# Six zero products in the opening of a fused attention and maxout kernel

## The chip, the cores and the metric

The kernel runs on one core of a Trainium2 chip. The metric is the device time of one execution in microseconds, the median of several runs. A core has five engines with a list of instructions each: TensorE (PE: matrix products into PSUM, with a weight load, PEld, ahead of each), VectorE (DVE), ScalarE (ACT), GpSimd (POOL) and SyncE (SP, which here issues the transfers). An engine works through its list in order and waits on semaphores for the others.

## The reference

Gated linear attention with a state of 48 x 48 for each head, and behind it a maxout layer; B, H, S, D = 4, 8, 768, 48:

```python
f = 1.0 / (1.0 + np.exp(-f_logit))
for t in range(S):
    state = f[:, :, t, :, None] * state + np.einsum('bhd,bhe->bhde', k[:, :, t], v[:, :, t])
    y[:, :, t] = np.einsum('bhd,bhde->bhe', q[:, :, t], state)
# x: y as 3072 tokens x 384
h1 = x @ w1            # 384 x 1024
h2 = x @ w2            # 384 x 1024
out = np.maximum(h1, h2) @ w_out   # 1024 x 384
```

## The kernel before

The 768 steps are cut into 3 windows of 256, and a piece is one window of one batch entry: 12 pieces, numbered 0 to 11. The steps inside a piece are turned into matrix products over chunks of 64. The maxout is computed as h2 + relu(h1 - h2), so the weights become wd = w1 - w2, and m2 = w2 @ w_out, worked out in the kernel itself, takes the place of h2 followed by w_out.

What runs when is written out by hand in the string ORDER. Each word is a step: letters for the kind, then the piece (and a part of it), then a letter for the engine (a ScalarE, v VectorE, p GpSimd, s SyncE), and after @ a PSUM bank or a slot of SBUF. The words are executed in order, and each engine's list holds its steps in that order. The waits are put in from what reads and writes the same bank or tile, so a product that rewrites a bank waits until the last reader of that bank is done.

The kinds that matter for the opening, with the line by which the profile names them:

- Lf, Lk, Lq, Lv: loads of f_logit, k, q, v of a piece (L124); Wa, Wb, Wo: loads of w1, w2, w_out (L137, L140, L144). All are issued by SP in ORDER's sequence.
- E, F, G: ScalarE's exp, ln, exp of the gate (L215 gate, L219 ell, L223 one); e: the sum of log gates in bf16 (L226).
- C: TensorE's running sum of e, one product of 384 columns (L230) and four of 2 columns (L233); X, Z: exp of it (L240, L245).
- i, j, K, Q, V: scaled k, q and the bf16 v (L249, L253, L260, L263; V, as all copies, is L113).
- t, u: TensorE's transposes of k and q (L278), U their copies out of PSUM (L113).
- A: scores of a piece, half at a time, 16 products (L315); m: VectorE's mask on them (L321).
- D: the state's addition, 32 products (L379); n, N: the state's update (L396, L398, L401).
- S, y: the two parts of the piece's output, from the state and from the masked scores (L336). Between them stands z (look, L113): a copy of one column of the banks that S wrote and that y adds into.
- Y: the output's copy xT (L113); wc, wt, wx: cast, transpose (L463) and copy of w2; wo: cast of w_out; wm: m2's 24 products (L478); wn its copies; ws: wd (L488).
- d: x times wd (L418), r: relu (L427), o: the last products (L440).

A kind h exists too, and ORDER does not use it. The tile zeros, a slot of SBUF that nothing else writes, is set to 0 at the start (L149):

```python
    zeros = slots[:, ZEROS, 0:256].bitcast(BF16)
    nc.vector.memset(slots[:, ZEROS, 0:256], 0.0)
...
    def step_h(n, b):
        for _ in range(n):
            nc.tensor.matmul(out=banks[:, b, :], lhsT=zeros[:, 0:C], rhs=zeros, start=True, stop=True)
```

The steps are then called by the words:

```python
    for word in ORDER.split():
        key, of, e, b = re.fullmatch(r"([A-Za-z]+)([0-9.]+)([avps]?)@?([0-9]*)", word).groups()
        steps[key](*map(int, of.split(".")), e, int(b or 0))
```

Of the kernel before, what the change touches and what calls it, by code (L numbers as in the profile page):

```python
# [17 lines left out]


ORDER = """  # L20
Lf1s@22 E1 F1 e1p Lf0s@14 E0 F0 Lk1s@10 C1@3 G1 e0v i1v Lq1s@3 C0@0 X1 Lq0s@23 Lv1s@17 V1p Z1 Z0 j1v Q1v
Lk0s@0 u1@2 Wb0s K1v Wb2s Wb1s t1@7 X0 G0 j0v i0p Lv0s@3 Q0v g2v U1.0a@7 D1@3 U1.1a@2 wc0a wc2p u0@7 Wo1s
n1.0@2 K0v U0.1v@7 Wo2s A1.0@1 m1.0@1 n1.1@2 wt0@3 t0@0 A1.1@1 wc1p wx0v@3 S1.0@6 Wo3s Wo0s wt2@4 Lf3s@16
m1.1@1 U0.0a@0 wt1@3 z1v@6 g0v wo1p V0a wo3p wx2a@4 A0.0@0 y1 m0.0@0 wx1a@3 wo2a S1.1@6 D0@0 n0.0@0 E3
A0.1@3 Wa1s n0.1@1 F3 Y1.0v@6 S0.0@4 Lf2s@11 Wa0s N1.1p wo0p m0.1@3 z0a@4 Lq2s@26 Lk3s@10 wm1@0 Y1.1a@7 e3v
wm3@0 wm2@0 wm0@0 y0 S0.1@4 Lq3s@22 Lk2s@19 wn2a@2 C3@2 ws2v g4p wn0a@0 Y0.1v@5 Y0.0a@4 ws3v E2 wn1v@1
Lf4s@3 Lv3s@24 Lf5s@15 d1.2@6 F2 e2v ws1v N0.1v ws0v Lv2s@0 d0.2@3 d0.3@4 d1.3@7 Z3 G3 r0.1a@3 j2v C2@5
d0.1@1 r1.1a@6 d1.1@4 Z2 X3 Q2v d1.0@3 V3p d0.0@0 r1.0a@3 i3v X2 K3v r0.0a@0 g6v G2 o1.0@6 Lq4s@4 j3v o0.0@4
Q3v u3@2 t3@2 i2v b1.0.0a@6 K2v u2@6 U3.2v@2 Lf6s@14 t2@6 b0.0.0v@4 o0.1@0 U2.0v@6 U2.1a@7 E4 D3@1 b0.1.0a@0
Lk5s@5 F4 n3.0@0 e4p A3.0@3 A3.1@6 o1.1@5 m3.0@3 E5 A2.1@0 S3.0@2 z3a@2 b1.1.0a@5 V2p m3.1@6 n3.1@0 A2.0@6  # L30
m2.0@6 y3 S3.1@2 D2@4 F5 Lk4s@15 n2.0@1 e5p C4@7 j4v Y3.2a@2 S2.0@5 Lq6s@8 g3v n2.1@2 Z4 Lv4s@9 Lq5s@2
m2.1@0 d3.1@2 G5 X4 Lf7s@23 z2a@5 Lk6s@0 G4 d3.2@3 g5p d3.3@4 y2 Q4p S2.1@5 C5@0 Lv5s@20 i4p d3.0@1 E6 F6
g1p Y2.2a@5 i5v Lf8s@26 r3.1v@3 Lq7s@27 e6v K4v Lk7s@7 d2.3@6 r3.0a@1 Lv6s@11 d2.2@5 X5 d2.0@2 j6v C6@1
d2.1@3 r2.1a@5 X6 V4a Lf9s@25 G6 u4@6 Z6 N3.1v t4@6 o3.1@4 U4.2v@6 D4@5 N2.1v r2.0a@2 Lv9s@15 A4.0@2 Z5
Lv7s@22 K5p j5v A4.1@0 o2.1@7 m4.0@2 Q5p b3.1.0a@4 E7 m4.1@0 F7 Lq8s@3 n4.0@1 i6p N4.0v V5a K6p b2.1.0a@7
n4.1@2 u5@2 t5@2 o2.0@4 G7 E8 U5.2v@2 F8 o3.0@5 S4.0@6 b3.0.0a@5 A5.0@2 z4v@6 Q6p m5.0@2 D5@0 S4.1@6
b2.0.0a@4 N4.1p y4 Lk9s@0 Y4.2a@6 Lk8s@20 A5.1@4 n5.0@2 e8p Lf10s@17 t6@2 u6@2 C8@0 m5.1@4 d4.1@7 N5.0p e7p
Lq10s@26 n5.1@0 d4.0@6 i7p X8 d4.3@1 Z8 r4.0a@6 U6.2v@2 j7v C7@3 Z7 V6p X7 Lv8s@6 d4.2@0 Lq9s@2 r4.1a@0
S5.0@6 E9 Lk11s@23 z5v@6 A6.0@4 D6@2 m6.0@4 F9 y5 n6.0@2 V7a K7p G9 N6.0v N5.1p S5.1@6 Lk10s@1 e9p A6.1@0 G8
o4.1@4 Y5.2v@6 d5.1@2 C9@7 b4.1.0a@4 m6.1@0 j8v d5.2@5 Q7p d5.3@6 d5.0@1 r5.0a@1 i8p E10 o4.0@0 n6.1@1  # L40
Lf11s@10 Lv10s@25 F10 r5.1v@5 G10 S6.0@1 K8p D7@4 z6v@1 n7.0@0 S6.1@1 g7p y6 u7@3 N7.0p Lq11s@17 t7@3 Q8v X9
Y6.2a@1 N6.1p Z9 b4.0.0a@0 Tk8s o5.0@6 n7.1@2 Tq8s e10v C10@5 V8v j9v d6.2@0 j10v U7.2a@3 Z10 d6.0@2
b5.0.0a@6 X10 d6.1@3 i9p r6.0a@2 d6.3@1 r6.1a@0 Q9v i10p Tq9s Q10v o5.1@4 K9v b5.1.0a@4 E11 A7.0@6 A7.1@0
D8@2 V9p S7.0@4 F11 m7.0@6 n8.0@0 o6.1@3 m7.1@0 V10p b6.1.0a@3 z7a@4 o6.0@2 b6.0.0a@2 D9@7 K10v Tk9s S7.1@4
y7 n9.0@1 D10@3 e11v A8.0@6 N9.0p Y7.2a@4 m8.0@6 A8.1@0 C11@2 d7.0@4 N7.1p d7.1@5 m8.1@0 X11 j11v d7.2@6 Z11
# [511 lines left out]
```

## Time and profile before

| what | before |
| --- | --- |
| median of 3 runs | 137.16 us |
| lowest and highest run | 136.89, 137.48 us |
| the profiled execution, its own time | 137.17 us |
| its span, first to last instruction | 135.4 us |
| busy in the span: PE / DVE / ACT / POOL | 120.2 / 95.6 / 83.8 / 53.5 us |
| weight loads (PEld), beside PE | 89.7 us |
| PE busy from 7 to 16 us, from 16 to 20, from 20 to 24 | 5.29 of 9, 4.00 of 4, 3.01 of 4 us |

Times in the profile count from the start of the span. PE's busy time merges overlapping products: a product's row runs from its start until its result is there, and the next one may start before. How fast a sequence of products goes is therefore read from one start to the next. A row of the timeline merges neighbours of a kind: the start, the time until the last one ends, the engine, the line, the output and inputs, the shape, how many, and in brackets the idle time before it with what ended that. The chain of waits follows the execution back from its last instruction, at each step to what released it.

### The profile page before, as it was taken

The page shows a single profiled execution, that of the slowest core. Times are in us where ns is not written, and L with a number is a line of the kernel's source. Part 1 is how long each engine was busy: PE and PEld are TensorE (multiplying, and loading weights), DVE is VectorE, ACT ScalarE, POOL GpSimd, SP SyncE. Part 2 cuts the span into 40 slices and gives each one's busy share as a digit, 9 for nine tenths or more (in the row PEclk, how much of TensorE's full clock was granted, in tenths as well). Part 3 has the DMA queues.
Part 4 walks back from the last instruction along what each step waited for, and adds up shares of the span by engine and source line. Part 5 has one row for each costly group of instructions (what it writes and reads, how often), then busy time and mean ns, then how long its engine had stood idle before and what let it go on. Part 6 is the DMA issues. An engine that isn't in the chain of part 4 may idle for free.

```text
span 135.4 us, 5468 instructions
## 1 busy us (share of the span) xinstructions
PE 120.2 (89%) x2415; PEld 89.7 (66%) x2415; DVE 95.6 (71%) x149; ACT 83.8 (62%) x132; POOL 53.5 (40%) x60
## 2 busy tenths in 40 slices
PE   0037797999999999999999999999999999999991
PEld 0016685667666788665977877667878677885570
DVE  6469885579998999988989949995894691030320
ACT  3693676399829699995689299863846012641421
POOL 5112552600012595399779976924291100000000
PEclk9999999999999999999999999999999999999999
DMA  3999999999999999999998999999929993020062
GB/s 96 273 261 294 392 356 337 320 345 241 251 262 268 263 259 250 266 261 248 250 238 207 278 262 236 249 160 204 110 82 228 389 351 134 0 116 0 18 242 94
DMA packets 62216, 30.77 MB, mean 227 GB/s; under 512 B 58736, under 2 KB 59120, under 8 KB 62192
## 3 DMA queue, kind: packets, MB, share of 16 engines
q1 hardware_dynamic: 62192, 30.41, 89.9%
q8 instruction: 19, 0.31, 1.0%
q14 instruction: 5, 0.04, 0.1%
HBM read 23.59 MB, written 4.72 MB: 209 GB/s over the span
## 4 chain that ended last, share of the span: by engine, by line
PE 79%; SPq 6%; DVE 6%; DMA 4%; ACT 2%; issue 1%; DVEq 0%
PE banks L440 33%; PE banks L418 22%; PE banks L336 9%; SPq L124 6%; DMA slots<-in_moe_w_dram 4%; PE banks L315 4%; PE banks L478 3%; DVE at_m L321 3%; PE banks L285 3%; PE banks L379 2%; ACT slots L113 2%; PE banks L230 2%; PE banks L463 1%; DVE wd L488 1%; PE banks L278 1%
## 5 line engine op out<-in xcount | busy, mean ns | idle before, releaser
L440 PE MATMUL banks<-wo,gT 128*128 128x384 bf16 (+1 forms) x200 | 35.2, 320 | 0.0
L418 PE MATMUL banks<-xT,wd 128*128 128x256 bf16 x288 | 34.1, 273 | 0.1
L321 DVE TENSOR_TENSOR at_m<-banks,mask 128x1024 bf16<-128x1024 f32 x24 | 28.9, 1218 | 3.1 <-PE banks L315 2.1
L418 PEld LDWEIGHTS <-wd 128*128 128x128 bf16 x288 | 27.1, 98 | 4.3 <-DVE wd L488 0.5
L440 PEld LDWEIGHTS <-gT 128*128 128x128 bf16 x200 | 19.1, 98 | 12.1 <-ACT gT L427 0.6
L427 ACT ACTIVATE gT<-banks 128x1024 bf16<-128x1024 f32 (+1 forms) x21 | 20.4, 985 | 9.1 <-PE banks L418 8.3
L113 ACT COPY slots<-banks 128x384 f32<-128x384 f32 (+2 forms) x22 | 11.2, 524 | 15.5 <-PE banks L440 15.4
L440 PE MATMUL banks<-m,xT 128*128 128x384 bf16 (+1 forms) x75 | 15.9, 321 | 0.1
L113 POOL CAST vb<-slots 128x768 bf16<-128x768 f32 x7 | 8.0, 1150 | 19.1 <-DMA slots<-in_v_dram 19.1
L429 DVE TENSOR_SCALAR gT<-banks 128x1024 bf16<-128x1024 f32 (+1 forms) x5 | 4.9, 1006 | 13.4 <-ACT slots L113 7.2
L215 ACT ACTIVATE gate<-slots 128x768 f32<-128x768 f32 x12 | 10.2, 846 | 5.1 <-DMA slots<-in_f_logit_dram 5.1
L249 POOL TENSOR_TENSOR slots<-slots,one 128x384 f32<-128x384 f32 x8 | 9.7, 1211 | 4.7 <-ACT one L223 2.6
L230 PE MATMUL banks<-e,u_inc 128*128 128x384 bf16 x12 | 4.3, 356 | 8.0 <-POOL e L226 7.4
L336 PE MATMUL banks<-at_m,vb 64*64 64x128 bf16 x576 | 10.7, 217 | 0.0
L219 ACT ACTIVATE ell<-gate 128x768 f32<-128x768 f32 x12 | 10.1, 846 | 0.5
L401 POOL TENSOR_TENSOR state<-tmp_s,dec 128x192 bf16<-128x192 f32 x10 | 5.9, 606 | 10.8 <-DVE tmp_s L396 10.8
L260 POOL TENSOR_TENSOR kp<-slots,inv 128x768 bf16<-128x768 f32 x5 | 9.1, 1815 | 2.6 <-ACT inv L240 1.5
L113 ACT COPY trs<-banks 128x1024 bf16<-128x1024 bf16 (+1 forms) x5 | 5.8, 1191 | 6.8 <-PE banks L278 4.3
L336 PEld LDWEIGHTS <-vb 64*64 64x64 bf16 x576 | 9.3, 106 | 0.5 <-issue 0.5
L336 PE MATMUL banks<-trs,state 48*64 48x128 bf16 x240 | 9.0, 222 | 0.3 <-DVE state L398 0.2
L315 PE MATMUL banks<-trs 48*64 48x128 bf16 x384 | 9.3, 225 | 0.0
L263 DVE TENSOR_TENSOR qp<-slots,dec 128x768 bf16<-128x768 f32 x8 | 9.0, 1136 | 0.3
(68 smaller groups left out, 178.2 us busy)
## 6 DMA issues: line engine op xcount, KB each, us to landing
slots<-in_f_logit_dram SPq DMA_DIRECT2D x12, 384.0 KB, 6.0
slots<-in_k_dram SPq DMA_DIRECT2D x12, 384.0 KB, 6.4
slots<-in_q_dram SPq DMA_DIRECT2D x12, 384.0 KB, 6.3
slots<-in_v_dram SPq DMA_DIRECT2D x12, 384.0 KB, 6.2
out_dram<-slots SPq DMA_DIRECT2D x11, 384.0 KB, 3.7
slots<-in_moe_w_dram SPq DMA_DIRECT2D x3, 512.0 KB, 6.0
slots<-in_moe_w_out_dram SPq DMA_DIRECT2D x4, 384.0 KB, 8.6
slots<-in_moe_w_dram SPq DMA_DIRECT2D x2, 768.0 KB, 7.4
```

The lines of the kernel that those rows point to most:

```text
L113: (nc.scalar.copy if e == "a" else engines[e].tensor_copy)(out, in_)
L215: nc.scalar.activation(flat(gate[s]), flat(loaded[s]["f"]), AF.Exp, bias=0.0, scale=-1.0)
L219: nc.scalar.activation(flat(ell[s]), flat(gate[s]), AF.Ln, bias=1.0, scale=1.0)
L249: engines[e].tensor_mul(even, even, one[s])
L260: engines[e].tensor_mul(pad("kp", s)[:, :, :, 0:D], by_parity(loaded[s]["k"]), both(inv[s]))
L263: engines[e].tensor_mul(pad("qp", s)[:, :, :, 0:D], by_parity(loaded[s]["q"]), both(dec[s][:, 0:HD].rearrange("p (h d) -> p h d", h=H)))
L315: nc.tensor.matmul(out=ps[h * HC:(h + 1) * HC, j % 2, par, :], lhsT=chunk(s, 0, rows, j, h)[:, par, :], rhs=chunk(s, 1, rows, j, h), start ...
L321: nc.vector.tensor_mul(at[s][:, jj].rearrange("p r j a t -> p (r j) (a t)"), banks[:, b:b + 2, :].rearrange("p r (j x) -> p (r j) x", j=2) ...
L336: nc.tensor.matmul(out=ys[s][h][c * DP:(c + 1) * DP, blk // 2, :], lhsT=lhs[:, at_col + off:at_col + off + DP], rhs=rhs, start=(s, h, c) n ...
L418: nc.tensor.matmul(out=ps[:, f, :], lhsT=wd[:, fp, kt, f * C:(f + 1) * C], rhs=xT[g][:, kt, :], start=(kt == 0), stop=(kt == KT - 1))
L427: nc.scalar.activation(dst, src, AF.Relu)
L440: nc.tensor.matmul(out=ps, lhsT=lhs, rhs=rhs[:, out_cols], start=(i == 0), stop=(i == len(terms) - 1))
```

## The change

ORDER gets three words more: h3@5 behind C0 (the first pieces' running sum), h1@5 behind t1 (the transposes of piece 1's k), and h2@5 behind A1.0 (the first half of piece 1's scores). Each is so many products of the zero tile with itself, 128 rows by 512 columns, into PSUM bank 5. No step reads what they write; bank 5 is written by S0.0 afterwards. The other words are the same in the same order, only broken into lines in another way:

```diff
-Lf1s@22 E1 F1 e1p Lf0s@14 E0 F0 Lk1s@10 C1@3 G1 e0v i1v Lq1s@3 C0@0 X1 Lq0s@23 Lv1s@17 V1p Z1 Z0 j1v Q1v
-Lk0s@0 u1@2 Wb0s K1v Wb2s Wb1s t1@7 X0 G0 j0v i0p Lv0s@3 Q0v g2v U1.0a@7 D1@3 U1.1a@2 wc0a wc2p u0@7 Wo1s
-n1.0@2 K0v U0.1v@7 Wo2s A1.0@1 m1.0@1 n1.1@2 wt0@3 t0@0 A1.1@1 wc1p wx0v@3 S1.0@6 Wo3s Wo0s wt2@4 Lf3s@16
...
+Lf1s@22 E1 F1 e1p Lf0s@14 E0 F0 Lk1s@10 C1@3 G1 e0v i1v Lq1s@3 C0@0 h3@5 X1 Lq0s@23 Lv1s@17 V1p Z1 Z0 j1v
+Q1v Lk0s@0 u1@2 Wb0s K1v Wb2s Wb1s t1@7 h1@5 X0 G0 j0v i0p Lv0s@3 Q0v g2v U1.0a@7 D1@3 U1.1a@2 wc0a wc2p
+u0@7 Wo1s n1.0@2 K0v U0.1v@7 Wo2s A1.0@1 h2@5 m1.0@1 n1.1@2 wt0@3 t0@0 A1.1@1 wc1p wx0v@3 S1.0@6 Wo3s Wo0s
...
```

Two of the three places, in TensorE's list. Behind t1, the transposes of kp (piece 1's k), D1 followed directly before, with a wait of its weight load for ScalarE and of its product for GpSimd's cast of v:

```order
L278 LDWEIGHTS kp_101
L278 MATMUL banks<-ident,kp_101 128x128
L379 LDWEIGHTS kp_101 [waits Activation_49]
L379 MATMUL banks<-vb_113,kp_101 64x48 [waits Pool_49]
L379 LDWEIGHTS kp_101
```

and now one zero product stands between them, with no wait of its own:

```order
L278 LDWEIGHTS kp_101
L278 MATMUL banks<-ident,kp_101 128x128
L492 LDWEIGHTS slots
L492 MATMUL banks<-slots 128x512
L379 LDWEIGHTS kp_101 [waits Activation_49]
L379 MATMUL banks<-vb_113,kp_101 64x48 [waits Pool_49]
```

Behind A1.0 (trs: the transposed k and q) the first transposes of w2 followed before, which wait for ScalarE's cast of w2 (slots) and for VectorE:

```order
L315 LDWEIGHTS trs_208
L315 MATMUL banks<-trs_208 64x128
L463 LDWEIGHTS slots [waits Activation_49]
L463 MATMUL banks<-ident,slots 128x128 [waits DVE_49]
L463 LDWEIGHTS slots
```

and now two zero products come first (the numbers behind the names of tiles are counted anew):

```order
L315 LDWEIGHTS trs_212
L315 MATMUL banks<-trs_212 64x128
L492 LDWEIGHTS slots
L492 MATMUL banks<-slots 128x512
L492 LDWEIGHTS slots
L492 MATMUL banks<-slots 128x512
L463 LDWEIGHTS slots [waits Activation_49]
L463 MATMUL banks<-ident,slots 128x128 [waits DVE_49]
```

The three behind C0 stand in the same way ahead of the first transposes of qp, which wait for VectorE. The lists of VectorE, ScalarE, GpSimd and SP hold the same steps in the same order as before.

More of the change, by code (lines that the diff above doesn't have):

```diff
@@ L20 @@
 ORDER = """
-Lf1s@22 E1 F1 e1p Lf0s@14 E0 F0 Lk1s@10 C1@3 G1 e0v i1v Lq1s@3 C0@0 X1 Lq0s@23 Lv1s@17 V1p Z1 Z0 j1v Q1v
-Lk0s@0 u1@2 Wb0s K1v Wb2s Wb1s t1@7 X0 G0 j0v i0p Lv0s@3 Q0v g2v U1.0a@7 D1@3 U1.1a@2 wc0a wc2p u0@7 Wo1s
-n1.0@2 K0v U0.1v@7 Wo2s A1.0@1 m1.0@1 n1.1@2 wt0@3 t0@0 A1.1@1 wc1p wx0v@3 S1.0@6 Wo3s Wo0s wt2@4 Lf3s@16
-m1.1@1 U0.0a@0 wt1@3 z1v@6 g0v wo1p V0a wo3p wx2a@4 A0.0@0 y1 m0.0@0 wx1a@3 wo2a S1.1@6 D0@0 n0.0@0 E3
-A0.1@3 Wa1s n0.1@1 F3 Y1.0v@6 S0.0@4 Lf2s@11 Wa0s N1.1p wo0p m0.1@3 z0a@4 Lq2s@26 Lk3s@10 wm1@0 Y1.1a@7 e3v
@@ L26 @@
[L26 to L40, printed above, removed]
@@ L41 @@
-Lf11s@10 Lv10s@25 F10 r5.1v@5 G10 S6.0@1 K8p D7@4 z6v@1 n7.0@0 S6.1@1 g7p y6 u7@3 N7.0p Lq11s@17 t7@3 Q8v X9
-Y6.2a@1 N6.1p Z9 b4.0.0a@0 Tk8s o5.0@6 n7.1@2 Tq8s e10v C10@5 V8v j9v d6.2@0 j10v U7.2a@3 Z10 d6.0@2
+Lf1s@22 E1 F1 e1p Lf0s@14 E0 F0 Lk1s@10 C1@3 G1 e0v i1v Lq1s@3 C0@0 h3@5 X1 Lq0s@23 Lv1s@17 V1p Z1 Z0 j1v
+Q1v Lk0s@0 u1@2 Wb0s K1v Wb2s Wb1s t1@7 h1@5 X0 G0 j0v i0p Lv0s@3 Q0v g2v U1.0a@7 D1@3 U1.1a@2 wc0a wc2p
+u0@7 Wo1s n1.0@2 K0v U0.1v@7 Wo2s A1.0@1 h2@5 m1.0@1 n1.1@2 wt0@3 t0@0 A1.1@1 wc1p wx0v@3 S1.0@6 Wo3s Wo0s
@@ new lines @@
+wt2@4 Lf3s@16 m1.1@1 U0.0a@0 wt1@3 z1v@6 g0v wo1p V0a wo3p wx2a@4 A0.0@0 y1 m0.0@0 wx1a@3 wo2a S1.1@6 D0@0
+n0.0@0 E3 A0.1@3 Wa1s n0.1@1 F3 Y1.0v@6 S0.0@4 Lf2s@11 Wa0s N1.1p wo0p m0.1@3 z0a@4 Lq2s@26 Lk3s@10 wm1@0
+Y1.1a@7 e3v wm3@0 wm2@0 wm0@0 y0 S0.1@4 Lq3s@22 Lk2s@19 wn2a@2 C3@2 ws2v g4p wn0a@0 Y0.1v@5 Y0.0a@4 ws3v E2
+wn1v@1 Lf4s@3 Lv3s@24 Lf5s@15 d1.2@6 F2 e2v ws1v N0.1v ws0v Lv2s@0 d0.2@3 d0.3@4 d1.3@7 Z3 G3 r0.1a@3 j2v
+C2@5 d0.1@1 r1.1a@6 d1.1@4 Z2 X3 Q2v d1.0@3 V3p d0.0@0 r1.0a@3 i3v X2 K3v r0.0a@0 g6v G2 o1.0@6 Lq4s@4 j3v
@@ new lines @@
+o0.0@4 Q3v u3@2 t3@2 i2v b1.0.0a@6 K2v u2@6 U3.2v@2 Lf6s@14 t2@6 b0.0.0v@4 o0.1@0 U2.0v@6 U2.1a@7 E4 D3@1
+b0.1.0a@0 Lk5s@5 F4 n3.0@0 e4p A3.0@3 A3.1@6 o1.1@5 m3.0@3 E5 A2.1@0 S3.0@2 z3a@2 b1.1.0a@5 V2p m3.1@6
+n3.1@0 A2.0@6 m2.0@6 y3 S3.1@2 D2@4 F5 Lk4s@15 n2.0@1 e5p C4@7 j4v Y3.2a@2 S2.0@5 Lq6s@8 g3v n2.1@2 Z4
+Lv4s@9 Lq5s@2 m2.1@0 d3.1@2 G5 X4 Lf7s@23 z2a@5 Lk6s@0 G4 d3.2@3 g5p d3.3@4 y2 Q4p S2.1@5 C5@0 Lv5s@20 i4p
+d3.0@1 E6 F6 g1p Y2.2a@5 i5v Lf8s@26 r3.1v@3 Lq7s@27 e6v K4v Lk7s@7 d2.3@6 r3.0a@1 Lv6s@11 d2.2@5 X5 d2.0@2
@@ new lines @@
+j6v C6@1 d2.1@3 r2.1a@5 X6 V4a Lf9s@25 G6 u4@6 Z6 N3.1v t4@6 o3.1@4 U4.2v@6 D4@5 N2.1v r2.0a@2 Lv9s@15
+A4.0@2 Z5 Lv7s@22 K5p j5v A4.1@0 o2.1@7 m4.0@2 Q5p b3.1.0a@4 E7 m4.1@0 F7 Lq8s@3 n4.0@1 i6p N4.0v V5a K6p
+b2.1.0a@7 n4.1@2 u5@2 t5@2 o2.0@4 G7 E8 U5.2v@2 F8 o3.0@5 S4.0@6 b3.0.0a@5 A5.0@2 z4v@6 Q6p m5.0@2 D5@0
+S4.1@6 b2.0.0a@4 N4.1p y4 Lk9s@0 Y4.2a@6 Lk8s@20 A5.1@4 n5.0@2 e8p Lf10s@17 t6@2 u6@2 C8@0 m5.1@4 d4.1@7
+N5.0p e7p Lq10s@26 n5.1@0 d4.0@6 i7p X8 d4.3@1 Z8 r4.0a@6 U6.2v@2 j7v C7@3 Z7 V6p X7 Lv8s@6 d4.2@0 Lq9s@2
@@ L43 @@
+r4.1a@0 S5.0@6 E9 Lk11s@23 z5v@6 A6.0@4 D6@2 m6.0@4 F9 y5 n6.0@2 V7a K7p G9 N6.0v N5.1p S5.1@6 Lk10s@1 e9p
+A6.1@0 G8 o4.1@4 Y5.2v@6 d5.1@2 C9@7 b4.1.0a@4 m6.1@0 j8v d5.2@5 Q7p d5.3@6 d5.0@1 r5.0a@1 i8p E10 o4.0@0
+n6.1@1 Lf11s@10 Lv10s@25 F10 r5.1v@5 G10 S6.0@1 K8p D7@4 z6v@1 n7.0@0 S6.1@1 g7p y6 u7@3 N7.0p Lq11s@17 t7@3
+Q8v X9 Y6.2a@1 N6.1p Z9 b4.0.0a@0 Tk8s o5.0@6 n7.1@2 Tq8s e10v C10@5 V8v j9v d6.2@0 j10v U7.2a@3 Z10 d6.0@2
 b5.0.0a@6 X10 d6.1@3 i9p r6.0a@2 d6.3@1 r6.1a@0 Q9v i10p Tq9s Q10v o5.1@4 K9v b5.1.0a@4 E11 A7.0@6 A7.1@0
```

## The prediction

> **What bounds the kernel now.** I read the page first, then the chain of waits, then the opening instruction by instruction, because the change touches nothing later.
>
> ```profile
> span 135.4 us, 5468 instructions
> ...
> PEclk9999999999999999999999999999999999999999
> ```
>
> The profiled execution took 137.17 us, 1.77 more than its span, and the runs' median is 137.16; a sum made on this span needs no correction. The clock row says full speed everywhere. Below, the durations contradict it for the opening.
>
> The chain of waits, from 14 to 33 us (start, length, what):
>
> ```profile
> 8.81 5.97 DMA slots<-in_moe_w_dram
> ...
> 15.97 1.03 PE banks L463 x8
> ...
> 20.79 1.24 DVE at_m L321
> 22.02 0.04 issue
> 22.07 0.33 PE banks L379 x17
> ...
> 23.76 4.01 PE banks L478 x24
> ...
> 29.26 0.56 DVE xT L113
> ...
> 31.62 0.88 DVE wd L488
> ```
>
> Until 15.97 a load of weights and its cast set the time, then TensorE (the transposes), then exchanges of VectorE and TensorE, then 24 products (L478), then VectorE up to 32.5. What follows is TensorE's. Busy time by stretch (stretch, its length, PE busy, the other engines, clock, DMA):
>
> ```profile
> 33.00:46.00 13.00, 13.00 (x258) 8.78 (x259) 11.89 (x18) 8.70 (x16) 2.61 (x3) 1.00 1.15 255
> 48.00:79.00 31.00, 30.72 (x684) 22.95 (x686) 27.75 (x35) 24.82 (x42) 25.17 (x22) 1.00 1.05 251
> 80.00:97.00 17.00, 17.00 (x357) 12.80 (x348) 14.98 (x19) 12.82 (x22) 9.24 (x9) 1.00 1.13 194
> 100.00:132.00 32.00, 32.00 (x490) 23.95 (x488) 12.60 (x19) 10.10 (x16) 2.54 (x3) 1.00 0.45 156
> ```
>
> PE idles 0.28 us in these 93. So the end moves by what the opening moves the products at 32.55, and by nothing else.
>
> Now TensorE in the opening (timeline: start, length, line, shapes, count, idle before):
>
> ```profile
> 8.49 0.48 PE L230 MATMUL banks<-e,u_inc 128*128 128x384 bf16 x1 [0.56 <-DVE e L226]
> ...
> 10.72 1.03 PE L278 MATMUL banks<-ident,qp 128*128 128x128 bf16 x8 [1.67 <-DVE qp L263]
> 11.60 1.04 PE L278 MATMUL banks<-ident,kp 128*128 128x128 bf16 x8
> 12.97 0.63 PE L379 MATMUL banks<-vb,kp 64*64 64x48 bf16 x32 [0.34 <-POOL vb L113]
> 13.79 1.03 PE L278 MATMUL banks<-ident,qp 128*128 128x128 bf16 x8 [0.19 <-DVE qp L263]
> 14.76 0.64 PE L315 MATMUL banks<-trs 48*64 48x128 bf16 x16
> 15.97 1.03 PE L463 MATMUL banks<-ident,slots 128*128 128x128 bf16 x8 [0.58 <-ACT slots L113]
> 16.80 1.06 PE L278 MATMUL banks<-ident,kp 128*128 128x128 bf16 x8
> 17.79 0.64 PE L315 MATMUL banks<-trs 48*64 48x128 bf16 x16
> ...
> 20.25 0.42 PE L315 MATMUL banks<-trs 48*64 48x128 bf16 x16
> ```
>
> The same 16 products of L315 take 0.64 us at 14.76 and 17.79, and 0.42 at 20.25. Eight transposes take 0.83 (15.97 to 16.80), or 0.104 each. TensorE runs slowly first. The rise lies late in the second group of L463: these stretches (that line alone) meet as many transposes in half the time.
>
> ```profile
> 19.50:19.90 0.40, 0.40 (x7) 0.40 (x5) 1.00 0.99 384
> 19.92:20.12 0.20, 0.20 (x7) 0.20 (x4) 1.00 1.52 543
> ```
>
> And PE alone, over two neighbouring stretches up to the rise:
>
> ```profile
> 13.09:16.50 3.41, 2.65 (x62) 1.00 1.01 402
> 16.50:19.92 3.42, 3.42 (x47) 1.00 1.12 343
> ```
>
> With holes (2.65 of 3.41) the clock did not rise; after an unbroken run, from 15.97, it did. That is the bound the traces give: an unbroken run of more than 1.9 us (10.72 to 12.64 was not enough) and at most 3.9.
>
> **The change, part by part.** Nothing is removed, no wait is added, no other engine's or queue's list changes. Added are six products of 512 columns, each with a weight load. No row has 512 columns; from the transposes, 128 columns slow are 0.104, so one costs 4 x 0.104 = 0.42 slow; from 24 products of 384 columns in 4.01 (0.167 each) one costs 0.22 fast.
>
> The three behind C0 start about 9.0 and end by 10.3, before the transposes at 10.72 that wait for VectorE: nothing. The one behind t1 runs from about 12.5 to 12.95; D1 behind it waits for GpSimd until 12.97: 0 to 0.2 late, and D1 would still end ahead of 13.79, where the next transposes wait for qp: nothing. The two behind A1.0 start at about 15.35 (its last products begin before 15.1 and end at 15.40). Slow they last until 16.2, so L463 starts 0.2 late; fast they end at 15.8, in the hole of 0.58. If the products leave the clock as it is, the sum is therefore +0.2.
>
> If they count as work, TensorE is busy from 10.72 on save the 0.19 before 13.79. An unbroken 3.9 us ends at 14.6 if that hole doesn't matter, at 17.7 if it starts the count anew. I follow the gain from there to 32.55, with these rows (all engines):
>
> ```profile
> 16.14 1.22 DVE L321 TENSOR_TENSOR at_m<-banks,mask 128x1024 bf16<-128x1024 f32 x1
> 17.54 0.68 DVE L113 COPY slots<-banks 128x1024 bf16<-128x1024 bf16 x1
> 18.48 1.23 DVE L321 TENSOR_TENSOR at_m<-banks,mask 128x1024 bf16<-128x1024 f32 x1 [0.27 <-PE banks L315]
> ...
> 23.26 0.83 POOL L113 CAST wo<-slots 128x768 bf16<-128x768 f32 x1 [2.56 <-DMA slots<-in_moe_w_out_dram]
> ...
> 25.72 0.84 ACT L215 ACTIVATE gate<-slots 128x768 f32<-128x768 f32 x1 [2.62 <-DMA slots<-in_f_logit_dram]
> 26.65 0.84 ACT L219 ACTIVATE ell<-gate 128x768 f32<-128x768 f32 x1
> 27.40 0.14 ACT L113 COPY look<-banks 128x1 f32<-128x1 f32 x1
> 27.53 0.56 DVE L226 TENSOR_TENSOR e<-ell 128x384 bf16<-128x384 f32 x1 [2.12 <-ACT look L113]
> 27.69 0.89 PE L336 MATMUL banks<-at_m,vb 64*64 64x128 bf16 x48
> 28.00 0.95 DVE L488 TENSOR_TENSOR wd<-slots 128x768 bf16<-128x768 f32 x1
> 28.69 0.34 PE L230 MATMUL banks<-e,u_inc 128*128 128x384 bf16 x1
> 29.26 0.56 DVE L113 CAST xT<-banks 128x384 bf16<-128x384 f32 x1 [0.30 <-PE banks L233]
> ```
>
> (1) The 16 transposes from 15.97 would save up to half of 1.7 us. But A1.1 (17.79) rewrites banks that m1.0 on VectorE reads until 17.36: it starts at 17.4, 0.4 earlier. (2) m1.1 (18.48) then follows the copy that ends at 18.22: 0.26 earlier, ending at 19.45. (3) A0.0 (20.25) writes a bank that m1.1 reads, so it starts at 19.5, 0.77 earlier; the transposes of wt2 and wt1, fast, are done by then. m0.0 (20.79), D0 (22.07) and the 24 products keep these 0.77: 22.9 instead of 23.69. (4) The second six need a cast that GpSimd begins when its load lands, 23.26 + 0.83 = 24.09. Unhindered they would start at 23.9; they start at 24.13. Gain left: 0.55; the products end at 27.2. (5) y0 (27.69) adds into the banks that look (ACT, 27.40) has to read first. Look stands in ScalarE's list behind gate and ell, which start when a load of f_logit lands at 25.7, issued at 15.3 and not moved by the change. So y0 goes on at 27.58: gain left 0.11. (6) Past it, VectorE's e waits for the same ell (27.49), and wd (28.00) stands behind e; wd ends at 28.95 as before. xT (29.26) is put down to the end of C3, whose products follow y0; with 0.11 off these, xT starts at 29.15. From there VectorE's list up to 31.62 + 0.88 has no idle place, and the products at 32.55 follow it: 0.11 earlier. If the 0.30 before xT has another cause, it is 0. I take 0.1, as the row names PE: 137.17 - 0.1 = 137.05, rounded. Of the 0.77 of step (3) a seventh is left, because one load decides at 25.7.
>
> The Trainium skill, in "TensorE: Matmul & The Clock Gate", Part 4, speaks against the change: a transpose does not count as work for the clock in the way that a product does. By it the zero products, with little but transposes between them, would raise nothing, which is the first rival. The rows bear it out poorly: the run in which the clock rose, 15.97 to 19.9, consists mostly of transposes. The same page, Part 1, says that the clock rises after one busy window of about 3.4 us, and that the windows run on freely; the two stretches above agree with it. By that rule the rise could come at a different moment in each execution, and the sum stays the same for all moments up to 17.7.
>
> **The rivals.** *No earlier rise.* The products do not count, or the holes still break the run. Then L463 starts 0.2 late and the chain passes it on through 20.79, 23.76 and 29.26: 137.17 + 0.2 = 137.4. For it: 2.65 of 3.41 busy was not enough, and the hole at 13.6 stays. Against: six products fill 1.3 us of holes, and the largest, 0.58, lies just ahead of the unbroken run, which then would start at 13.79.
>
> *The load is not the bound in other executions.* y0 waits for look by only 0.15 (27.54 to 27.69). Should f_logit land 0.5 us earlier in an execution that isn't profiled, steps (5) and (6) give way and the 0.55 of step (4) comes through: 137.17 - 0.55 = 136.6. The runs' spread, 136.89 to 137.48, is of such a size; against it, the profiled execution lies on the median.
>
> *Slower: the clock falls back.* Faster products leave more idle time between 16 and 23, since VectorE's times stay. From the point where some 3.4 us hold too little work, the clock drops again, and the 24 products meet it: half speed over 3.4 us loses 1.7 of work. Less the 0.55 gained, y0 starts 1.15 later: 138.3. Against it, the holes of 0.5, 0.24 and 0.2 us between 21.5 and 23.4 do not slow the products behind them now.
>
> **How the numbers follow.** The forecast, 137.05, has 0.62; no earlier rise 0.17; the load not binding 0.14; the fall 0.05; 0.02 is left for what I do not see. A measurement of this kernel tells a difference from none at about 0.5%, 0.69 us. The forecast and the first rival lie inside; of the second some lies beyond, where all 0.77 of step (3) survive. That makes 0.86 for no difference, 0.07 faster, 0.07 slower. The range is the first rival's 137.4 and the second's 136.6, each with about 0.1 for the spread of a median: 136.5 to 137.5. The forecast's own range, 0 to 0.11 gained and the same spread, is 136.95 to 137.3.
>
> **What would show it.** Right: L315 at 14.76 or at 17.4 takes about 0.42, the 24 products of L478 begin near 22.9 and pause near 24, gate still begins at 25.7 behind its load, and wd at 28.0 and L418 at 32.5 stand where they stood. Step (1) is wrong if L315 still takes 0.64 at its second place; step (5) if y0 begins before look has ended or gate begins earlier; step (6) if xT keeps its 0.30. The forecast falls if the L418 products at 32.55 move by more than 0.4 either way, or if PE idles after 33.

## The result, and the profile after

The change made the kernel slower: 138.03 us (137.69 to 138.35) against 137.09 (136.84 to 137.48) in runs on the same chip, a ratio of 1.007 with a 95% interval of 1.0054 to 1.0087. The profiled execution took 137.69 us, 0.52 more than that of before. Of two kernels below the profiled execution was disturbed: that of the change with padding had a mean granted clock of 0.988, and that of the change run again took 413.23 us, its L440 products 0.88 us each instead of 0.32 although the granted clock reads 1.00, so it is not read; ratios leave such runs out. The head of the page of after, with the row of the queue that loads instructions:

```profile
span 135.9 us, 5480 instructions
...
PEclk9999999999999999999999999999999999999998
...
q8 instruction: 19, 0.31, 0.9%
```

The span grew by 0.5 us, and there are 12 instructions more: six products, each with its weight load. The clock row says full speed, as before, but for the last of its 40 slices.

The chain of waits of after in the opening (start, length, what):

```profile
15.35 10.27 DMA slots<-in_f_logit_dram
...
25.64 0.85 ACT gate L215
...
27.32 0.14 ACT look L113
...
29.06 0.56 DVE xT L113
...
31.42 0.88 DVE wd L488
...
32.35 1.70 PE banks L418 x14
```

The load of f_logit now sets the opening, and the products that began at 32.55 begin at 32.35. The opening is 0.20 us faster. So the loss lies behind it. Busy time by stretch of after, in the same columns as before:

```profile
33.00:46.00 13.00, 12.99 (x271) 8.80 (x273) 11.88 (x18) 8.76 (x16) 2.60 (x3) 1.00 1.20 258
48.00:79.00 31.00, 30.91 (x723) 23.18 (x723) 27.67 (x37) 25.24 (x42) 25.18 (x22) 1.00 1.10 259
80.00:97.00 17.00, 17.00 (x343) 12.68 (x344) 15.24 (x19) 12.81 (x22) 7.30 (x10) 1.00 1.16 189
100.00:132.00 32.00, 31.07 (x480) 22.98 (x479) 12.68 (x18) 9.74 (x15) 1.13 (x2) 1.00 0.44 154
```

From 48 to 79 TensorE is busy for 30.91 us instead of 30.72, and from 100 to 132 for 31.07 instead of 32.00. The second is the loss. TensorE's timeline there, of before and then of after (start, length, line, shapes, count, idle before):

```profile
110.13 0.87 PE L336 MATMUL banks<-at_m,vb 64*64 64x128 bf16 x48
...
110.97 0.87 PE L336 MATMUL banks<-at_m,vb 64*64 64x128 bf16 x48
...
112.61 0.65 PE L440 MATMUL banks<-m,xT 128*128 128x384 bf16 x3
113.09 1.46 PE L440 MATMUL banks<-wo,gT 128*128 128x384 bf16 x8
114.39 1.80 PE L418 MATMUL banks<-xT,wd 128*128 128x256 bf16 x15
```

```profile
109.51 0.87 PE L336 MATMUL banks<-at_m,vb 64*64 64x128 bf16 x48
...
110.36 0.87 PE L336 MATMUL banks<-at_m,vb 64*64 64x128 bf16 x48
...
111.99 0.65 PE L440 MATMUL banks<-m,xT 128*128 128x384 bf16 x3
113.58 1.47 PE L440 MATMUL banks<-wo,gT 128*128 128x384 bf16 x8 [0.93 <-issue]
114.89 1.36 PE L418 MATMUL banks<-xT,wd 128*128 128x256 bf16 x11
```

At 110 the work stands 0.62 us earlier than before; after one pause it stands 0.49 later. Read from start to start the pause costs 1.11 us (0.93 as idle time, since the row of a product ends only with its result). The 0.62 is made of the opening's 0.20 and of 0.42 for the second of two pauses that the kernel before had and this execution has not (0.28 as idle time; the first lies in the opening):

```profile
22.64 0.31 PE L379 MATMUL banks<-vb,kp 64*64 64x48 bf16 x15 [0.24 <-issue]
...
71.03 0.21 PE L379 MATMUL banks<-vb,kp 64*64 64x48 bf16 x2 [0.28 <-issue]
```

That gain of 0.42 is not shown to come from the change: two kernels below whose list is the same up to there (before with o8.1 moved, and the six tiny products late) do not pause at that place. Sum: -0.62 + 1.11 = +0.49, against +0.52 measured. The waits of after between 90 and 135 us (engine, line, releaser; total, times, longest) name no engine and no load for the pause:

```profile
PEld L440 <- issue: 1.3, 1, 1.3
...
PE banks L440 <- issue: 0.9, 1, 0.9
```

"issue" means that nothing the profile shows was waited for.

**Where the pauses lie.** Counting TensorE's instructions in the order of its list, the pause of after lies at instruction 4546. The pauses by "issue" of before lie at 450 (0.24 us at 22.40) and at 2498 (0.28 at 70.75). Each is 194 plus a multiple of 256. Such a place is called a border below. The page's row of q8 says why that number matters: 19 packets of 0.31 MB in all are 16 KB each, and TensorE's list of 4841 instructions (4853 after) has 19 borders, from 194 to 4802; the padded kernels below, with 256 instructions more than before, have 20 packets. So I took them for loads of TensorE's code, one block of 256 instructions each. The DMA view, cut to a tenth of a microsecond, shows the one of this place. It starts between 111.5 and 111.6 us before (first row), and between 111.1 and 111.2 after (second row):

```profile
q8 instruction: 1, 0.02, 61.3%
```

```profile
q8 instruction: 1, 0.02, 68.2%
```

The share is of 16 engines over 0.1 us, so the packets took 0.613 x 1.6 = 0.98 us and 0.682 x 1.6 = 1.09 us.

**Code theory.** At this place, TensorE crosses a border; the next block's load starts 1.2 to 2.0 us later, takes 0.9 to 1.2, and 1.2 to 1.5 us after that its instructions run. If TensorE has used up the block that it is in before that, it pauses. Two pieces' products of L336 stand close together near 110, 132 products (264 instructions) in some 2 us. Twelve more instructions ahead put the border nine products behind this run, where before it lay fifteen behind it. At that border:

| kernel | border 4290 crossed | load | border 4546 reached | resumed | from crossing to reaching |
| --- | --- | --- | --- | --- | --- |
| before | 110.14 | 111.50 to 112.48 | 113.91 | 113.98 | 3.77 us |
| after | 109.46 | 111.19 to 112.28 | 112.32 | 113.57 | 2.86 us |

Before, the code came just in time: 112.48 + 1.50 = 113.98. After, it could be used at 112.28 + 1.29 = 113.57, 1.25 us too late. That is a reading of one execution of each, so it was tested.

### The profile page after: what moved, and what is told of

Read it like the earlier page. It is cut to its first block, busy times and chain, and to the rows that moved or that the text cites. A ratio compares the mean times of both kernels' runs of the same rounds, so it can differ in the third digit from the quotient of the medians.

```text
span 135.9 us, 5480 instructions
## 1 busy us (share of the span) xinstructions
PE 120.3 (89%) x2421; PEld 88.0 (65%) x2421; DVE 96.7 (71%) x149; ACT 83.6 (61%) x132; POOL 51.3 (38%) x60
## 4 chain that ended last, share of the span: by engine, by line
PE 71%; DMA 12%; DVE 8%; ACT 3%; SPq 2%; issue 2%; DVEq 0%; ACTq 0%
PE banks L440 33%; PE banks L418 22%; DMA slots<-in_f_logit_dram 8%; PE banks L336 7%; DMA slots<-in_q_dram 4%; PE banks L315 3%; PE banks L285 3%; DVE at_m L321 2%; DVE qp L263 2%; PE banks L379 2%; SPq L124 2%; PE banks L230 1%; DVE wd L488 1%; DVE slots L253 1%; SPq L144 1%
## 5 line engine op out<-in xcount | busy, mean ns | idle before, releaser
L440 PE MATMUL banks<-wo,gT 128*128 128x384 bf16 (+1 forms) x200 | 35.2, 320 | 0.9 <-issue 0.9
L418 PE MATMUL banks<-xT,wd 128*128 128x256 bf16 x288 | 34.0, 273 | 0.2
L418 PEld LDWEIGHTS <-wd 128*128 128x128 bf16 x288 | 27.1, 98 | 4.3 <-DVE wd L488 0.5
L440 PEld LDWEIGHTS <-gT 128*128 128x128 bf16 x200 | 19.0, 98 | 13.3 <-issue 1.3
L440 PE MATMUL banks<-m,xT 128*128 128x384 bf16 (+1 forms) x75 | 15.9, 321 | 0.1
L113 POOL CAST vb<-slots 128x768 bf16<-128x768 f32 x7 | 6.4, 914 | 20.2 <-DMA slots<-in_v_dram 20.2
L336 PE MATMUL banks<-at_m,vb 64*64 64x128 bf16 x576 | 11.0, 217 | 0.2 <-ACT look L113 0.2
L249 POOL TENSOR_TENSOR slots<-slots,one 128x384 f32<-128x384 f32 x8 | 9.1, 1133 | 4.0 <-ACT one L223 2.6
L336 PEld LDWEIGHTS <-vb 64*64 64x64 bf16 x576 | 9.5, 106 | 0.9 <-issue 0.9
L263 DVE TENSOR_TENSOR qp<-slots,dec 128x768 bf16<-128x768 f32 x8 | 9.5, 1199 | 0.3
L253 DVE SCALAR_TENSOR_TENSOR slots<-gate,slots 128x384 f32<-128x384 f32 x12 | 9.5, 794 | 0.1
L315 PE MATMUL banks<-trs 48*64 48x128 bf16 x384 | 9.1, 218 | 0.4 <-DVE at_m L321 0.4
```

Of the source, the lines that this page charges most:

```text
L113: (nc.scalar.copy if e == "a" else engines[e].tensor_copy)(out, in_)
L249: engines[e].tensor_mul(even, even, one[s])
L253: engines[e].scalar_tensor_tensor(out=even, in0=gate[s][:, :, 1, :], scalar=1.0, in1=even, op0=ALU.add, op1=ALU.mult)
L263: engines[e].tensor_mul(pad("qp", s)[:, :, :, 0:D], by_parity(loaded[s]["q"]), both(dec[s][:, 0:HD].rearrange("p (h d) -> p h d", h=H)))
L315: nc.tensor.matmul(out=ps[h * HC:(h + 1) * HC, j % 2, par, :], lhsT=chunk(s, 0, rows, j, h)[:, par, :], rhs=chunk(s, 1, rows, j, h), start ...
L336: nc.tensor.matmul(out=ys[s][h][c * DP:(c + 1) * DP, blk // 2, :], lhsT=lhs[:, at_col + off:at_col + off + DP], rhs=rhs, start=(s, h, c) n ...
```

## The experiments

The rival theories were these. The opening's clock: faster products early, or the products' power, cost something later. The pause: a chance of one execution. The work: six products cost their own time. All zero products below write to places that nothing reads, so nothing is left out of the computation unless it is said.

**The same number of instructions, no work.** The six products of 512 columns become six of 2 columns.

```diff
-... C0@0 h3@5 ... t1@7 h1@5 ... A1.0@1 h2@5 ...
+... C0@0 ht3@5 ... t1@7 ht1@5 ... A1.0@1 ht2@5 ...
+    def step_ht(n, b):
+        for _ in range(n):
+            nc.tensor.matmul(out=banks[:, b, 0:2], lhsT=zeros[:, 0:C], rhs=zeros[:, 0:2], start=True, stop=True)
```

> The six products stay in their three places but have 2 columns instead of 512: the same 12 instructions in TensorE's list, almost no work. Code theory (the 12 instructions move the point at which the next 16 KB of TensorE's code is needed to just behind the dense run of L336 near 110 us, and the code isn't there yet): the idle place of about 1 us near 113 us, put down to issue, stays; the clock rises where it did before, between 18.7 and 20.3 us; time 137.8 to 138.4. Work theory (the six products' work, or what the earlier clock changes in the order of transfers, causes it): no such idle place, 137.1 within 0.3.

Measured: 138.26 us, ratio 1.006 (1.0031 to 1.0088): the whole loss. Its timeline:

```profile
18.63 1.89 PE L463 MATMUL banks<-ident,slots 128*128 128x128 bf16 x16
...
114.17 1.48 PE L440 MATMUL banks<-wo,gT 128*128 128x384 bf16 x8 [0.99 <-issue]
```

The 16 transposes of L463 take 1.89 us here (1.32 in after, at 17.98), so the early rise of the clock is gone, and the pause is as long as in after. Neither the work of the products nor the clock makes the loss.

**Three products instead of six**, the three behind C0.

```diff
-... t1@7 h1@5 X0 ... A1.0@1 h2@5 m1.0@1 ...
+... t1@7 X0 ... A1.0@1 m1.0@1 ...
```

> Only the three zero products behind C0: 6 instructions. Code theory: the border near 113 us moves by half as much; about 0.5 us of idle time there, in some executions nearly none, 137.2 to 137.7. The clock should rise at about 12.2 us as in the change if these three products suffice for it; with the rise at 16.5 or later the other three are needed. Work theory: with half of the added work about half of the loss or all of it, but no relation to the place near 113.

Measured: 138.02 us, ratio 1.0042 (1.001 to 1.0074). The pause is the one expected; the median is longer than the 137.2 to 137.7 expected, and the profiled execution, 137.50, is not.

```profile
17.79 0.64 PE L315 MATMUL banks<-trs 48*64 48x128 bf16 x16
...
113.87 0.99 PE L440 MATMUL banks<-wo,gT 128*128 128x384 bf16 x5 [0.48 <-issue]
```

With six instructions added the pause is 0.48, about half, and the second L315 still takes 0.64: no early rise.

**The tiny products late.** Six of them right ahead of S11.0, near 109 us; the opening is that of before.

```diff
-... m11.1@6 b8.0.0v@5 S11.0@3 ...
+... m11.1@6 b8.0.0v@5 ht6@3 S11.0@3 ...
```

> The kernel before, with six products of 2 columns (12 instructions) directly ahead of S11.0, near 109 us; the opening is untouched. Code theory: only the last code borders move, the one near 113 by the same 12 instructions, so about 1 us of idle there, 137.8 to 138.3 where before has 137.1 to 137.3. If the loss came from the opening instead (loads, clock, order of waits), no such idle place and the time of before.

Measured: 138.13 us, ratio 1.0063 (1.0032 to 1.0093).

```profile
113.70 1.48 PE L440 MATMUL banks<-wo,gT 128*128 128x384 bf16 x8 [0.49 <-issue]
```

The loss needs nothing in the opening. The pause at the same product is half of what was expected, since the load started sooner after the border here (1.25 us, where after has 1.73).

**Twice as many tiny products** in the opening: ht6, ht2, ht4 for h3, h1, h2.

> Twelve products of 2 columns in the opening (24 instructions), in the three places of the change. Code theory: the border near 113 comes 12 instructions earlier than with six, which is six products of L418 at 0.13 us, so TensorE arrives 0.8 earlier at the same code: idle place of 1.5 to 1.9 us where six gave 0.99 and three 0.48; time 0.6 to 0.9 longer than with six. If the idle place does not grow with the number of instructions, the code's position is not what sets it.

Measured: 138.21 us, ratio 1.007 (1.0043 to 1.0097). The profiled execution took 138.87.

```profile
50.20 0.86 PE L336 MATMUL banks<-at_m,vb 64*64 64x128 bf16 x45 [0.23 <-issue]
...
113.95 0.50 PE L418 MATMUL banks<-xT,wd 128*128 128x256 bf16 x3 [1.31 <-issue]
```

The pause grows to 1.31, less than the 1.5 to 1.9 expected, and stands where 24 instructions put the border, in L418. The median, though, is no longer than with six: a miss. One execution shows 138.87; why the others are shorter I do not know.

**The place eased.** One step of the dense part moved: o8.1 (11 products of 384 columns) ahead of y11, so that the block holds more work; once with the change and once without.

```diff
-S10.1@0 z11a@3 y11 O6.2s S11.1@3 Y10.2a@0 d9.2@5 o8.1@7 d9.3@6 ...
+S10.1@0 z11a@3 o8.1@7 y11 O6.2s S11.1@3 Y10.2a@0 d9.2@5 d9.3@6 ...
```

> The change, with o8.1 (11 products of L440, 1.8 us) moved from behind the dense run of L336 into its middle, ahead of y11. The 256 instructions of that block of code then take about 3.9 us instead of 2.9. Code theory: the idle place near 113 falls from 0.93 to below 0.2; what the opening and the moved borders near 22 and 70 us gained (0.2 and 0.28 in the profiles) comes through: 136.6 to 137.2, at or a little below before. If the idle place stays, or comes up elsewhere, 137.7 to 138.3.

> The kernel before with the same move of o8.1 and no zero products, to tell the move's own worth from that of the change. Its border near 113 was met in time by 0.1 us already: 136.9 to 137.3, no difference from before within 0.3; the difference between this run and the change with the move is what the six zero products give when the code is no obstacle: 0 to 0.5.

Measured: with the change 137.87 us, ratio 1.0045 (1.0019 to 1.0072); without it 137.44, ratio 1.002 (0.9995 to 1.0044). The change with the move has this pause, and its profiled execution took 137.29:

```profile
113.64 0.24 PE L336 MATMUL banks<-trs,state 48*64 48x128 bf16 x2 [0.27 <-issue]
```

The pause shrinks from 0.93 to 0.27, and the profiled execution by 0.40, but the median does not follow (expected 136.6 to 137.2): a miss for the time. Against the kernel before with the same move, the six products should have given 0 to 0.5; the median is 0.43 longer with them, the profiled execution 0.05 (137.29 to 137.24).

**A whole block of padding.** If all shifts by 256 instructions, the borders lie where they lay before. So 128 tiny products were put at the very start of before, and 122 at the start of the change (with its 12 instructions 256 in all).

```diff
-Lf1s@22 E1 F1 ...
+Lf1s@22 ht128@5 E1 F1 ...
```

> The kernel before, with 128 products of 2 columns ahead of TensorE's first product: 256 instructions, no zero products of 512 columns. Both theories: the time of before, 137.1 within 0.3, with L418's second group at 32.5. If it is slower by 0.5 or more, the additional instructions or the additional load of code cost something by themselves, and the run before it in this list has to be read against this one; if it is faster, the products at the start raise the clock.

> The change as it is, and 122 products of 2 columns ahead of TensorE's first product, where it is idle until 7.4 us: together 256 instructions more than before, one whole block of code, so that every block border falls on the instruction on which it fell before. Code theory: no idle place near 113, the earlier products at 32.5 (0.2 earlier in the change's profile) come through: 136.6 to 137.1. Work theory: the idle place stays, 137.8 to 138.4.

Measured: before with padding 138.95 us, ratio 1.012 (1.0073 to 1.0166); the change with padding 138.13 in the five executions with a granted clock of 1.00, ratio 1.0085 (1.0045 to 1.0125), and 141.26 over all twelve. Both times were expected near 137. Neither profiled execution pauses at the product where after has its pause, which comes near 116 and 118 us in them. But they pause at other borders, the first for 0.65 at 69.29, the second for 1.09 at 24.17 and 1.15 at 55.17, and the padding has a price of its own, which makes the pair useless as a clean test of time. In the padded kernel before, the DMA view from 6 to 7 us and the chain of waits show:

```profile
q8 instruction: 1, 0.02, 7.6%
```

```profile
2.86 7.43 DMA slots<-in_q_dram
...
10.32 0.57 DVE slots L253
```

and in after the same VectorE instruction stands here:

```profile
9.10 0.56 DVE L253 SCALAR_TENSOR_TENSOR slots<-gate,slots 128x384 f32<-128x384 f32 x1
```

A load of code now falls among the first loads of data, 0.076 x 16 = 1.2 us long; the first q lands in time for 10.32 instead of 9.10, and the products that begin at 32.55 in before begin at 34.51. The padded change has such a load from 5.64 us, and that instruction at 10.02; the other twelve executions have no load of code before 18 us, and it at 8.88 to 9.14. Whether the load or the many tiny products make q late was not told apart. The padded change's profile shows one more thing:

```profile
24.17 0.31 PE L379 MATMUL banks<-vb,kp 64*64 64x48 bf16 x15 [1.09 <-issue]
...
25.25 5.67 PE L478 MATMUL banks<-wo,slots 128*128 128x384 bf16 x24
```

After a pause of 1.09 us at a border the 24 products take 5.67 us instead of the 4.01 of before, and the granted clock of that page reads five tenths in the slice from 24.5 to 28.0. That is a loss like the one that the prediction's third rival described, but not in the change itself, and no run shows that the pause brought it about.

**The shift undone.** This is the deciding test. The change keeps its six products in the opening, and six products of L336 with their weight loads are left out of piece 8 near 104 us, so every instruction behind them has its old number again. That part of the output is then not computed. The same six are left out of before, for the worth of the work, and a third kernel leaves six out of piece 2 near 50 us instead.

```diff
     def step_y(s):
...
                     for h in range(2):
+                        if s == 8 and j == 1 and par == 0:
+                            continue
```

> The change, with six products of piece 8's second part of the output (near 104 us) and their six weight loads left out; that part of the output is not computed. So every instruction of TensorE behind them has the number again that it has before the change, while the opening keeps its six zero products. Left-out work: 48 such products go from 109.51 to 110.19, 0.014 us each, so 0.09 us in all. Code theory: the pause of 0.93 us at 112.6 is gone (below 0.1), and the time is that of the change less 0.93 less 0.09, near 136.7 in the profiled execution, 0.99 to 1.00 of the kernel before. Rival, the loss comes from the opening's products themselves (work, clock, a state of buffers) and the pause only happens to lie there: the pause stays, or appears elsewhere, and the time is 138.0 less 0.09, near 137.9.

> The kernel before with the same six products of piece 8 left out (that part of the output is not computed). It gives the worth of what the other kernel leaves out, and moves TensorE's instructions behind 104 us the other way, 12 numbers lower than before. Code theory: the border of the block that was reached just in time at 113.9 falls 12 instructions later in the work, so no pause appears there, and the time is that of before less 0.09 us, 137.0 to 137.2. Rival, any change of the count by 12 disturbs: a pause of 0.3 us or more, and 137.5 or more.

> The change, with six products of the same kind left out already in piece 2 (near 47 us) instead of piece 8. All later instructions have the numbers of before. Code theory: the pause of 0.28 us at 70.8, which the kernel before had and the change had not, comes back, and the one at 112.6 is gone; time near 136.7 + 0.28 = 137.0. Rival: the pause at 112.6 stays and 70.8 stays clear, near 137.9.

> The change itself once more, to see how far the pause varies from one profiled execution to the other. Code theory: a pause at 112 to 114 again, of 0.5 to 1.3 us, and a median of 138.0, 1.004 to 1.009 of before. Rival, that the pause was a chance of one execution: none, with a time that still is near 138.0, so that the loss lies elsewhere.

Measured, all on one chip beside before at 137.27 us:

| kernel | median | ratio to before | 95% interval | pause at 112 to 114 |
| --- | --- | --- | --- | --- |
| the change again | 137.92 us | 1.0045 | 1.0018 to 1.0073 | not read, see above |
| the change, six left out at 104 us | 137.10 us | 0.9977 | 0.9947 to 1.0006 | none |
| the change, six left out at 50 us | 137.21 us | 0.9995 | 0.9969 to 1.0021 | 0.03 us |
| before, six left out at 104 us | 137.01 us | 0.9984 | 0.9963 to 1.0004 | none |

The kernel with six left out at 104 us:

```profile
18.61 0.42 PE L315 MATMUL banks<-trs 48*64 48x128 bf16 x16
...
50.43 0.75 PE L336 MATMUL banks<-at_m,vb 64*64 64x128 bf16 x37 [0.45 <-issue]
```

```profile
100.00:132.00 32.00, 32.00 (x489) 23.89 (x487) 12.71 (x19) 9.90 (x16) 2.65 (x3) 1.00 0.44 154
```

TensorE is busy for all 32.00 us again. The median is 0.82 us below that of the change, of which the left-out work explains 0.09, by 48 such products in 0.68 us. So 0.7 us come from the numbers of the instructions alone. The ratio lies where the theory put it; the profiled time, 137.46, does not (136.7), since it has a pause of 0.45 at 50.

The third kernel's expectation was half wrong. The pause at 113 is gone, but the one at 70.8 did not come back; this execution pauses at 50 instead:

```profile
50.49 0.63 PE L336 MATMUL banks<-at_m,vb 64*64 64x128 bf16 x29 [0.40 <-issue]
```

So does the kernel of before with six left out, which has these two rows; both places lie at borders, 450 and 1474, and the products left out come later than either:

```profile
22.64 0.31 PE L381 MATMUL banks<-vb,kp 64*64 64x48 bf16 x15 [0.84 <-issue]
...
50.66 0.66 PE L336 MATMUL banks<-at_m,vb 64*64 64x128 bf16 x32 [0.40 <-issue]
```

At these borders the code comes just in time in some executions and late in others. At 4546 the profiles agree with the count: all six kernels with instructions added ahead of it pause there for 0.27 us or more, and none of the five without does for more than 0.03. For that border, with the time from crossing 4290 to reaching 4546, and the time from that crossing until the code of the next block ran or could have run (start of the load, its length, and the 1.2 to 1.5 us behind it):

| kernel, instructions added ahead of the border | TensorE's time for the block | code needed | pause |
| --- | --- | --- | --- |
| before, 0 | 3.77 us | 3.84 us | none |
| before, o8.1 moved, 0 | 4.18 us | in time | none |
| change, six left out at 104 us, 0 | 3.93 us | in time | none |
| change, six left out at 50 us, 0 | 4.12 us | in time | 0.03 us |
| before, six left out at 104 us, 12 fewer | 4.47 us | in time | none |
| three zero products, 6 | 3.28 us | 4.08 us | 0.48 us |
| six tiny, late, 12 | 2.85 us | 3.67 us | 0.49 us |
| the change, o8.1 moved, 12 | 3.72 us | 4.20 us | 0.27 us |
| the change, 12 | 2.86 us | 4.11 us | 0.93 us |
| six tiny, 12 | 2.86 us | 4.17 us | 0.99 us |
| twelve tiny, 24 | 2.19 us | 3.77 us | 1.31 us |

In each row with a pause of 0.27 us or more it is the difference of the two columns less 0.2 to 0.3 us, the part of it that the last products' own length covers. That "code needed" varies from 3.67 to 4.20 is mostly the start of the load, 1.25 to 1.90 us after the crossing; what sets it was not found.

How fast TensorE goes through a block does not decide alone. In the kernel before, it goes through the 128 products from border 1986 to border 2242 in 1.68 us and does not pause; the load for 2242 starts at 62.91, 1.25 us ahead of the crossing of 1986 (first the stretch of TensorE, which also counts two products begun just ahead of it, then the DMA view from 62.9 to 63.0 us):

```profile
64.16:65.80 1.64, 1.64 (x130) 1.00 1.13 280
```

```profile
q8 instruction: 1, 0.02, 57.1%
```

In the padded kernel before, the same products take 1.69 us, their load starts only 0.24 ahead of the crossing, and the pause of 0.65 at 69.29 follows. Over all borders of the 13 executions read, the load starts between 2.1 us ahead of the crossing and 4.2 behind it. Alike is what follows its end: no block begins sooner than 1.2 us after its load has ended, and each pause at a border named here ends 1.2 to 1.6 us after the end of a load. That is why the pauses are read as waits for code, though no run moves a load by itself.

## Why the prediction was wrong

The forecast was 137.05 us and no measurable difference, the range 136.5 to 137.5. Measured was 138.03, slower by 0.7%. By the prediction's own steps:

**The step that failed** stands in its first part: "PE idles 0.28 us in these 93. So the end moves by what the opening moves the products at 32.55, and by nothing else." After 33 us TensorE indeed has hardly any hole, and no other engine's list changes. But the added instructions have a place in TensorE's list, and the list is loaded in blocks whose borders moved. The 0.93 us of idle time at 112.6, 1.11 from start to start, are not in the sum at all; its price for an instruction was only the time that its product takes. Two rows could have told: the 0.28 us of idle time, which the prediction counted without asking for its releaser (it is "issue"), and q8 with its 19 packets, a queue that it did not look at. All three rivals played in the opening, and none could give this. The prediction did name the sign of its own failure: "if PE idles after 33".

The Trainium skill, in "Runtime: NRT & Kernel Launch", "Instruction fetch mechanics", describes it: an engine's code comes in blocks of 16 KiB, 256 instructions, fetched by its sequencer while the block before runs, and the cost of a crossing is mostly hidden. The trace agrees with the blocks (19 packets of 16 KB, pauses that lie multiples of 256 apart). It also agrees with "mostly" by count, with one pause at a border in after and two in before; but what was not hidden is 0.93 us in the change, and 0.27 to 1.31 in its variants at the same border.

**The opening, steps (1) to (6), went nearly as worked out.** TensorE's timeline of after:

```profile
14.53 0.42 PE L315 MATMUL banks<-trs 48*64 48x128 bf16 x16
14.88 0.60 PE L492 MATMUL banks<-slots 128*128 128x512 bf16 x2
16.02 0.62 PE L463 MATMUL banks<-ident,slots 128*128 128x128 bf16 x8 [0.54 <-ACT slots L113]
...
17.46 0.42 PE L315 MATMUL banks<-trs 48*64 48x128 bf16 x16 [0.37 <-DVE at_m L321]
...
19.23 0.64 PE L315 MATMUL banks<-trs 48*64 48x128 bf16 x16
...
22.46 1.15 PE L478 MATMUL banks<-wo,slots 128*128 128x384 bf16 x6
24.06 3.09 PE L478 MATMUL banks<-wo,slots 128*128 128x384 bf16 x18 [0.45 <-POOL wo L113]
...
27.52 0.87 PE L336 MATMUL banks<-at_m,vb 64*64 64x128 bf16 x47 [0.20 <-ACT look L113]
```

- (1) L315 takes 0.42 at 14.53, so the clock had risen by then. A1.1 starts at 17.46 (said 17.4) and waits for VectorE's at_m, as said.
- (2), (3) A0.0 starts at 19.23 (said 19.5), L478 at 22.46 (said 22.9): in this execution there was more to gain than 0.77. (The 0.64 of the group at 19.23 is no slow clock: its products take 0.21 to 0.24 each, as in the groups of 0.42, and the second starts 0.2 late.)
- (4) The 24 products pause for GpSimd's cast, from 23.61 to 24.06 (said "near 24").
- (5) gate begins at 25.64 behind its load, look ends at 27.46, y0 goes on at 27.52 (said 25.7 and 27.58). One load indeed takes back nearly all of the gain.
- (6) L418 begins at 32.35, 0.20 earlier; said was 0.11. The idle time before xT falls from 0.30 to 0.18, and it is now put down to ScalarE's part of xT, which follows look, and not to TensorE:

```profile
29.06 0.56 DVE L113 CAST xT<-banks 128x384 bf16<-128x384 f32 x1 [0.18 <-ACT xT L113]
```

The gain holds over the profiles: that group of L418 begins between 32.22 and 32.51 in the four with the six whole products, and between 32.49 and 32.57 in the six with none or tiny ones, the padded kernels and the change run again left out. It is too small for the median to show.

**The rivals.** *No earlier rise* did not come. The second L315 takes 0.42 in all four profiles with six whole products (the padded kernel and the change run again left out), and 0.56 to 0.64 in those with none, with tiny ones or with three. The rise came by 14.5 us in after, and only later in the other three, whose first L315 still takes 0.64; so its moment varies between executions, as the prediction held possible. *The load is not the bound* did not come either; gate waits for it. *The clock falls back*: the change itself shows no sign of it between 16 and 33 us; the padded change does, with its cause open.

**The chances.** 0.86 for no difference left 0.07 for slower, and the only mechanism named for it, with 0.05, lies in the opening. What the opening moves at 32.5 was priced to 0.1 us, since one load takes back whatever the steps before it gain. What was missing is a whole term.

**What stays open.** The medians of the change, and of the change with o8.1 moved, lie 0.3 and 0.6 us above their profiled executions (138.03 to 137.69, 137.87 to 137.29). Only profiled executions show their pauses, and the change's own pause is read in one, so it is not shown where the others lose that. What sets the start of a load of code is open too, and with it why the same border brings a pause in one execution and none in another. No kernel here beats before: with the shift undone the change is at 0.9977, with part of the output left out, and before with the same left out at 0.9984.

## What to carry to other kernels

An instruction added to an engine's list costs its own time and also moves all code behind it against the borders of its blocks. Where an engine works for a hundred microseconds without a hole, look for the stretches in which it goes through 256 instructions in a few microseconds, and for the ends of the instruction queue's loads in the DMA view: here no block began sooner than 1.2 us after the end of its load, and at border 4546 a block needed 3.7 to 4.2 us from the crossing before. A run of many small products is where a few instructions more or less can decide. A pause that is put down to "issue", at a place that fits 256 instructions, is the sign of it in a profile; the same word stands at places that do not fit, as for 0.33 us at 16.35 in the change with six left out at 104 us, where the record of one of two zero products is missing. Leaving out as many instructions elsewhere is a cheap test.

## What the runs showed of the hardware

- TensorE's code came in 19 loads of 16 KB, one for each border. At border 4546 blocks used up in 2.19 to 3.28 us were followed by pauses of 0.48 to 1.31 us; at border 2242 a block used up in 1.68 us was not, since its load had started 1.25 us ahead.
- At all borders of 13 executions, no block began sooner than 1.2 us after the end of its load.
- Six products of 2 columns cost 0.6% of the time (138.26 us), about as much as six of 512 columns (0.7%): not their work but their number in the list cost it.
- In the two executions with a load of code at 5.6 to 6.6 us and many tiny products ahead, the first q was taken up at 10.02 and 10.32 us instead of 8.88 to 9.14.
- Zero products brought the clock up earlier by different amounts in different executions: the whole of L315's first place was fast in one of four, its second place in all four.
